# Opening of a fused attention and feed-forward kernel: queries begun on half of the contraction and half of the tokens, eight heads kept in float32 until their shift arrives

## The chip, the cores and the metric

One Trainium2 chip, one core. The metric is the device time of the whole kernel in microseconds (us). Runs of one kernel mostly agree within 0.2 us. A run also has a mean granted TensorE clock, where 1.000 means full clock throughout; it does not count the half-rate stretch at the very start.

PE is TensorE's matmul side and PEld its weight loads, DVE is VectorE, ACT is ScalarE, POOL is GpSimd, SP is the engine that issues the loads. "Head 4" means the fifth head; heads are counted from 0.

## The reference

Layer norm with a scale and a shift computed from a conditioning vector, attention of 32 query heads over the last 512 cached keys (4 key groups), a projection, a gated residual, then the same frame round a SwiGLU feed-forward. What matters here is the first line:

```python
mod = (silu(c) @ w_mod)            # six rows of 1024: sa (shift), ca (scale), ga, sb, cb, gb
h = layernorm(x) * (1 + ca) + sa
q = (h @ wq)                       # 2048 tokens, D = 1024, 32 heads of 128
p = softmax(q @ k.T * 128 ** -0.5) # 512 keys
x = x + ga * ((p @ v) @ wo)
# ... then h = layernorm(x) * (1 + cb) + sb, silu(h @ w_gate) * (h @ w_up) @ w_down, gated by gb
```

## The kernel before

The first 512 tokens can't be projected before the scale `ca` is there, and `ca` and `sa` must be computed from 2 MB of weights each. So the kernel transposes the normalised tokens, scales them, projects them without the shift, and adds `sa @ wq` (a "bias" per head) at the eviction. The kernel before does this for heads 0 to 3; the later heads read tokens that have had the shift added.

The contraction of 1024 runs in eight slices of 128 (`DT = 8`, `HK = 4`). `mm` is the only helper that issues matmuls, so nearly all matmuls have its line, L268, in every profile. `warm(n, b)` issues n dummy matmuls of 512 columns into bank b, which keep the TensorE clock up. The Trainium skill ("TensorE: Matmul & The Clock Gate", Part 1) says why one would: the array starts at half clock, goes to full after a busy window of some 3.4 us, and goes back after an idle one.

```python
            # ... x0..x3, all of the scale weights, wq group 0, shift weights, k0, wq group 1, ... are loaded in this order
            warm(7, WB)
            x_first(0)                         # transposes of 128 tokens, 8 slices
            warm(5, WB)
            x_first(1)
            for k in range(3):
                mod_ca(k)                      # 8 single-column matmuls: scale columns
                warm(1, WB)
            # ... x_first(2), x_first(3), mod_ca(3..7) with dummies between
            x_mod()                            # all 8 slices scaled, 512 tokens each, on DVE and ACT

            QB0 = [PVB, PVB + 1, SCB, QB]      # banks 5, 6, 0, 4
            for kc in range(DT):
                for h in range(LEAD + 1):      # heads 0 to 3
                    mm(bank(QB0[h]), wq_s[0][:, kc, h * P:(h + 1) * P], hT[0][:, kc, :], kc == 0, kc == DT - 1, ...)
                # ... shift columns mod_sa(0), mod_sa(1) after slices 3 and 6
            # ... mod_sa(2), dummies, mod_sa(3), key transposes of group 0, dummies
            for h in range(LEAD + 1):          # bias of heads 0 to 3, single columns
                for kc in range(DT):
                    mm(bank(SCB + 2, 1, 2 * h), wq_s[0][:, kc, h * P:(h + 1) * P], mod_bf[:, kc:kc + 1], ...)
            warm(5, SCB + 3)
            # ... shift added to the 8 slices; heads 0 to 3 evicted with their bias
```

The head loop, one turn per head. In these traces PE's matmuls come in the order of the program.

```python
            for i in range(1, NA + 2):
                # ... loads; key transposes of group i-1 in turns 2 to 4
                if i + LEAD < NA:
                    if i == 1:
                        scores(0)              # 4 matmuls into banks 0 to 3; ACT: 2 exponentials read them
                    qproj(i + LEAD, ...)       # 8 matmuls of 512 columns
                # ... in turns 7 to 14 one slice of another modulation column
                if 1 <= i - 1 < NA:
                    scores(i - 1)
                if 0 <= i - 2 < NA:
                    pv(i - 2)                  # 16 matmuls of 129 columns
```

Tracking: `T.op(engine, emit, reads, writes)` puts in a wait for the last write of each buffer it reads, whatever part of that buffer was written.

The softmax here doesn't subtract the row's maximum and nothing guards it: scores larger than these inputs give would overflow.

## Time and profile before

| | |
|---|---|
| Median of three runs | 1277.83 us (1277.81 to 1279.52) |
| Profiled run | 1279.7 us, span 1277.9 us, clock 1.000 |
| First query matmul, first scores, first exponential (profile) | 16.77, 29.24, 29.87 us |

Lines of the profile page of the kernel before: busy times of the engines with their share of the span, and the chain of work that ended last.

```profile
PE 1271.0 (99%) x7656; PEld 646.3 (51%) x7656; DVE 477.2 (37%) x883; ACT 340.3 (27%) x385; POOL 42.2 (3%) x102
...
PE 99%; DVE 0%; DMA 0%; ACT 0%; issue 0%; ACTq 0%
```

PE is the chain, so only PE time counts. A "busy" PE includes dummies and matmuls at half clock.

Lines of the timeline of the kernel before: start, duration, engine, line, operation, what it writes and reads, count, and in brackets how long the engine was idle before and what ended that.

```profile
8.77 0.15 PEld L268 LDWEIGHTS ps<-arena 128*128 128x128 bf16 x1 [0.28 <-issue]
...
9.20 0.15 PEld L268 LDWEIGHTS ps<-arena 128*128 128x128 bf16 x1 [0.28 <-issue]
...
16.77 3.89 PE L268 MATMUL ps<-arena 128*128 128x512 bf16 x16 [0.36 <-DVE arena L468]
...
29.24 1.02 PE L268 MATMUL ps<-arena 128*128 128x512 bf16 x4 [0.35 <-DVE arena L663]
...
29.87 1.02 ACT L690 ACTIVATE arena<-ps 128x1024 bf16<-128x1024 f32 x1 [0.26 <-PE ps L268]
```

At 9 us the dummies still start 0.43 us apart, which is half clock. Queries begin at 16.77 us and the first scores at 29.24 us.

### The profile page before, as it was taken

How to read it: one execution, taken by the hardware profiler on the slowest of the kernel's cores; microseconds unless marked ns; L12 is line 12 of the kernel's file. 1: busy time of each engine (PE TensorE's matmuls, PEld its weight loads, DVE VectorE, ACT ScalarE, POOL GpSimd, SP SyncE). 2: the span in 40 equal slices, each digit the busy share in tenths (PEclk: the TensorE clock that was granted, in tenths of full speed). 3: DMA queues.
4: the chain of work that ended last, by engine and by line, in shares of the span. 5: the costliest groups of instructions: out<-in, count | busy, mean ns of one | idle time of the engine just before them, and what ended most of it. 6: DMA issues, size and time to landing. Idle time of an engine off the chain costs nothing.

```text
span 1277.9 us, 17862 instructions
## 1 busy us (share of the span) xinstructions
PE 1271.0 (99%) x7656; PEld 646.3 (51%) x7656; DVE 477.2 (37%) x883; ACT 340.3 (27%) x385; POOL 42.2 (3%) x102
## 2 busy tenths in 40 slices
PE   8999999999999999999999999999999999999999
PEld 4565545555455564466544444444444444444444
DVE  3555324765247652265422322233222331222222
ACT  3555303555025550055510111011100111011100
POOL 1011000000000010000000000000000000000000
PEclk9999999999999999999999999999999999999999
DMA  9999403977018741065352964055421654035200
GB/s 319 234 239 235 104 1 72 200 139 165 3 22 186 153 104 42 2 131 112 71 149 81 291 221 132 23 145 162 134 72 45 197 146 132 17 114 166 67 9 25
DMA packets 234830, 155.31 MB, mean 122 GB/s; under 512 B 129024, under 2 KB 220032, under 8 KB 234752
## 3 DMA queue, kind: packets, MB, share of 16 engines
q1 hardware_dynamic: 176496, 95.45, 31.2%
q10 hardware_dynamic: 58256, 58.73, 14.6%
q8 instruction: 60, 0.98, 0.3%
q14 instruction: 18, 0.15, 0.1%
HBM read 119.54 MB, written 4.19 MB: 97 GB/s over the span
## 4 chain that ended last, share of the span: by engine, by line
PE 99%; DVE 0%; DMA 0%; ACT 0%; issue 0%; ACTq 0%
PE ps L268 99%; PE ps L272 0%; DMA x_res<-in_A_x_dram 0%; DVE st L396 0%; DVE arena L663 0%; ACT arena L471 0%; DVE arena L468 0%; DVE tmp L730 0%; DVE arena L732 0%; DVE nsc L407 0%; DVE mv L493 0%; DVE gain L448 0%; DVE mod_bf L462 0%; DVE bq L669 0%; ACTq L79 0%
## 5 line engine op out<-in xcount | busy, mean ns | idle before, releaser
L268 PE MATMUL ps<-arena 128*128 128x512 bf16 (+2 forms) x7383 | 1265.7, 334 | 3.0 <-POOL arena L389 2.2
L268 PEld LDWEIGHTS ps<-arena 128*128 128x128 bf16 x7383 | 636.1, 98 | 621.0 <-issue 3.5
L690 ACT ACTIVATE arena<-ps 128x1024 bf16<-128x1024 f32 x256 | 262.2, 1024 | 354.6 <-PE ps L268 343.0
L915 ACT ACTIVATE arena<-ps 128x512 bf16<-128x512 f32 x112 | 66.9, 597 | 506.4 <-PE ps L268 506.4
L916 DVE TENSOR_TENSOR arena<-ps,arena 128x512 bf16<-128x512 f32 x112 | 77.5, 692 | 276.2 <-PE ps L268 276.2
L730 DVE TENSOR_TENSOR tmp<-ps,rowb 128x512 f32<-128x512 f32 (+1 forms) x65 | 44.4, 683 | 319.1 <-PE ps L268 319.1
L609 DVE CAST arena<-ps 128x512 bf16<-128x512 f32 x124 | 85.8, 692 | 57.1 <-PE ps L268 57.1
L711 DVE TENSOR_TENSOR arena<-ps,rl 128x512 bf16<-128x512 f32 x128 | 88.5, 691 | 4.7 <-DVE rl L708 0.2
L708 DVE RECIPROCAL rl<-ps 128x4 f32<-128x4 f32 x128 | 23.3, 182 | 120.5 <-PE ps L268 120.5
L396 DVE BATCH_NORM_STATS2 st<-x_res 128x6 f32<-128x512 bf16 x62 | 42.3, 683 | 4.0 <-DMA x_res<-in_A_x_dram 3.8
L401 POOL TENSOR_SCALAR rstd<-mv 128x1 f32<-128x1 f32 x28 | 6.2, 222 | 895.6 <-DVE mv L400 895.6
L563 DVE SCALAR_TENSOR_TENSOR arena<-arena 128x1024 bf16<-128x1024 bf16 x24 | 29.1, 1215 | 0.0
L732 DVE TENSOR_TENSOR arena<-tmp,x_res 128x512 bf16<-128x512 f32 (+1 forms) x33 | 22.3, 676 | 1.1
L732 DVE TENSOR_TENSOR x_res<-tmp,x_res 128x512 bf16<-128x512 f32 x32 | 22.1, 692 | 1.1
L412 DVE TENSOR_SCALAR arena<-arena,gain,mod_bf 128x512 bf16<-128x512 bf16 x56 | 20.3, 405 | 0.0
L407 DVE TENSOR_SCALAR nsc<-x_res,mv,rstd 128x1024 bf16<-128x1024 bf16 x30 | 16.0, 534 | 0.0
L403 POOL TENSOR_TENSOR rstd<-rstd,mhalf 128x1 f32<-128x1 f32 x28 | 15.8, 565 | 2.3
L578 POOL TENSOR_SCALAR arena<-arena,c 128x128 bf16<-128x128 bf16 x24 | 14.4, 620 | 32.7 <-PE ps L268 32.4
L268 PEld LDWEIGHTS ps<-sc_bf,arena 128*128 128x128 bf16 x192 | 7.4, 97 | 3.4
L268 PE MATMUL ps<-sc_bf,arena 128*128 128x1 bf16 x192 | 7.5, 164 | 0.0
L400 DVE BATCH_NORM_AGGREGATE mv<-st 128x2 f32<-128x12 f32 x28 | 5.8, 208 | 1.0
L272 PE MATMUL ps<-arena,nsc 128*128 128x128 bf16 x16 | 2.1, 312 | 1.1 <-DVE nsc L407 1.1
(53 smaller groups left out, 42.7 us busy)
## 6 DMA issues: line engine op xcount, KB each, us to landing
arena<-in_A_wq_dram SPq DMA_DIRECT2D x31, 1024.0 KB, 5.7
arena<-in_B_w_gate_dram ACTq DMA_DIRECT2D x28, 1024.0 KB, 5.5
arena<-in_B_w_up_dram ACTq DMA_DIRECT2D x28, 1024.0 KB, 8.2
arena<-in_A_wo_dram SPq DMA_DIRECT2D x8, 1024.0 KB, 7.0
arena<-in_B_w_down_dram SPq DMA_DIRECT2D x7, 1024.0 KB, 8.1
out_dram<-arena SPq DMA_DIRECT2D x15, 256.0 KB, 2.0
x_res<-in_A_x_dram SPq DMA_DIRECT2D x3, 1024.0 KB, 7.9
arena<-in_w_mod_dram SPq DMA_DIRECT2D x8, 256.0 KB, 6.1
```

What stands on the lines that cost most here:

```text
L268: T.op(PE, lambda: TE.matmul(out_ap, lhsT, rhs, start=start, stop=stop, skip_group_check=skip), reads=reads, writes=[bank_buf])
L396: T.op(DVE, lambda: V.bn_stats(st_[sl][:, hf * 6:hf * 6 + 6], x_res[:, t, hf * 512:hf * 512 + 512]), reads=[B_x[t]], writes=[B_st[sl]])
L412: T.op(DVE, lambda: V.tensor_scalar(dst[:, dt, :], dst[:, dt, :], gain[gi][:, dt:dt + 1], mod_bf[:, ccol + dt:ccol + dt + 1], op0=ALU.mult ...
L563: T.op(DVE, lambda: V.scalar_tensor_tensor(mt[n % 2], mt[n % 2], 1.0, sc_row, op0=ALU.mult, op1=ALU.mult, accum_out=mcol[:, n:n + 1]), rea ...
L609: T.op(DVE, lambda: V.tensor_copy(qT_s[qs], bank(b)), writes=[PB[b], B_qT[qs]])
L690: T.op(ACT, lambda: A.activation(ex_s[es][:, 2 * kp:2 * kp + 2, :], banks2(SCB + 2 * kp), AF.Exp, scale=att_scale), writes=[PB[SCB + 2 * k ...
L708: T.op(DVE, lambda: V.reciprocal(rl[r][:, :].rearrange("p (a b) -> p a b", a=2), psap(PVB * 512 + P, [[512, 2], [130, 2]])), writes=both + ...
L711: T.op(DVE, lambda: V.tensor_tensor(o_s[os_].rearrange("p (a b) d -> p a b d", a=2), psap(PVB * 512, [[512, 2], [130, 2], [1, P]]), rlb, A ...
L730: T.op(DVE, lambda: V.tensor_tensor(tmp[s][:, 0:n], bank(b, n), rowb[ri][:, c0:c0 + n], ALU.mult), reads=[B_row[ri]], writes=[PB[b], B_tmp ...
L732: T.op(DVE, lambda: V.tensor_tensor(dst[:, c0:c0 + n], tmp[s][:, 0:n], x_res[:, t, c0:c0 + n], ALU.add), reads=[B_tmp[s], B_x[t]], writes= ...
L915: T.op(ACT, lambda: A.activation(sg_s[ss], bank(gb), AF.Silu), writes=[PB[gb], B_sg[ss]])
L916: T.op(DVE, lambda: V.tensor_tensor(guT[:, ft, :], bank(ub), sg_s[ss], ALU.mult), reads=[B_sg[ss]], writes=[PB[ub], B_gu[ft]])
```

## The change

Its intent is to begin real work earlier and to use the wait for the shift for projections, not for dummies.

- The scale weights come in two halves of the columns (1 MB each). The first half is enough for slices 0 to 3.
- Tokens 0 to 255 are scaled and projected (heads 0 to 2, slices 0 to 3) while tokens 256 to 511 are still being normalised.
- Heads 0 to 7 are projected without the shift. Each leaves PSUM as float32 (`q_raw`), and gets its bias in SBUF (`q_shifted`) when the shift column is there.
- Bias columns of heads 0 and 1 come before the first scores, those of heads 2 to 7 after them.
- In turns 2 to 8, heads 8 to 11 are projected in every second turn, as four projections are already done. Four slices of the next modulation column are moved into turn 7, which has no projection.
- Dummies fall from 35 to 19. A third query-weight slot takes group 2 early.

The diff, cut to its core:

```diff
-            for k in range(DT):
-                T.op(dq("q_wca%d" % k), lambda: SP.dma_start(wca[k], w_mod[k * P:(k + 1) * P, D:2 * D]), writes=[B_wca[k]])
+            def load_wca(hf):      # half of the columns, in four loads
...
-            warm(7, WB)
+            warm(12, WB)
             x_first(0)
-            warm(5, WB)
+            warm(3, WB)
+            for k in range(4):
+                mod_ca(0, k)
             x_first(1)
...
+            x_first(2, 0, HK)
+            x_gain(0)
+            x_mod(0, 0, 2 * P)
+            norm_last(0, 512)
+            norm(2, 2, 2, 512, 512)
...
+            BB = SCB + 3
+            QB0 = [QB, PVB, PVB + 1, SCB, SCB + 1, SCB + 2, QB, PVB]
+            def q_raw(h):          # float32 eviction to SBUF, DVE or ACT in turn
+            def q_bias_mm(h0, h1): # single columns into bank BB, then one copy to bq
+            def q_shifted(h):      # qT = qf + bq
...
+            for kc in range(HK):
+                for h in range(3):
+                    q_first(h, kc, 0, 2 * P)
+                if kc == 2:
+                    x_first(tl, 0, HK)
+                    x_mod(0, 2 * P, 2 * P)
+                    norm_last(512, 512)
+            for k in range(4):
+                mod_ca(1, k)
+            for kc in range(HK):
+                for h in range(3):
+                    q_first(h, kc, 2 * P, 2 * P)
+            x_first(2, HK, HK)
+            x_first(tl, HK, HK)
+            for k in range(4, DT):
+                mod_ca(1, k)
+            x_gain(1)
+            x_mod(1, 0, CH)
+            # ... head 3, slices 4 to 7 of heads 0 to 3, heads 4 to 7, with mod_sa and key transposes between
+            q_bias_mm(0, 2)
+            # ...
                     if i == 1:
                         scores(0)
-                    qproj(i + LEAD, PVB if i == 2 else QB)
+                        q_bias_mm(2, NQ0)
+                    if i > NQ0:
+                        qproj(i + LEAD)
+                    elif i % 2 == 0:
+                        qproj(NQ0 - 1 + i // 2)
```

## The prediction

> **What bounds the kernel.** The engine table gives PE 99% of a 1277.9 us span (DVE 37%, ACT 27%), and the chain that ended last is PE for 99%. So only PE time counts, and the change touches only the opening, before the ninth head. The timeline there: first transposes at 7.5 us, first query matmul at 16.77, first scores at 29.24. Query work in that stretch is 4 heads x 8 matmuls x 0.213 = 6.8 us. Much of the rest is dummies: 35 warming matmuls in the old prologue. From 29.24 on PE is gapless: heads take about 3.5 us each (3.7 to 3.9 with a key transpose or gate column), while ACT's two exponentials take 2.14.
>
> **What the change does.** It starts queries on half the contraction and half the tokens, so they need only half of the scale columns (1 MB loaded, not 2), and fills the wait for the shift column with heads 4 to 7 instead of dummies (19 left, not 35). It adds 8 float32 evictions (about 0.69 us each, split over DVE and ACT, off PE), 8 SBUF additions and 32 more single-column bias matmuls (16 of them take 0.40 us: 25 ns each, 0.8 us).
>
> **Estimated opening.** The DMA stretches hold 350 to 390 GB/s from 6 to 27 us; in the new order the first half of the scale should land near 10 us (the fourth of these loads now lands at about 10, the last near 12.7), the first query weights near 11.5, the shift columns by about 25. First query matmul: about 12 instead of 16.8, with gaps until about 16.5, as each half waits for DVE and ACT to scale it. Then 16 + 32 dense matmuls and the shift columns: first scores at about 29 to 30, as before, but with 8 heads projected. Worth 4 x 1.71 = 6.8 us.
>
> **Given back.** (1) Bias columns of heads 2 to 7: 48 x 25 ns = 1.2 us after the first scores. (2) They go to PSUM bank 3, which those scores have just filled: they wait until both exponentials (2 x 1.02 us) have read it, and PE has nothing else in order: about 1.7 us idle. (3) Heads 2 to 8 project only every second turn; a turn without it (1.75 us of scores and values) is shorter than 2.14 of ACT: some 0.5 us in all. (4) The keys of the second group come behind 1 MB more of weights, at about 32 us, when they are wanted: 0 to 1 us. About 6.8 - 3.4 - slips = 3 us left.
>
> **Prediction.** 1274.6 us; 8 in 10: 1271.5 to 1278.5. The rest (gate, up, down) doesn't change.
>
> **Clock.** In this trace matmuls of 512 columns start 0.43 us apart until about 11 us, 0.21 after. The Trainium skill ("TensorE: Matmul & The Clock Gate", Part 1) says the array starts at half rate and goes to full after a busy window of some 3.4 us; the trace agrees. Twelve dummies in a row without the present 1.1 us gap should bring full rate by 8 to 10 us. But the new stretch from 10 to 17 us is thin (short matmuls, waits, few dummies); should it fall back to half rate, the gain is gone.
>
> **What would show it.** Timeline: first query matmul near 12, first scores near 29 to 30; a PE gap of 1.5 to 2 us right after the first four score matmuls, released by the exponential; gaps of 0.2 to 0.5 us in odd turns until head 8; nothing different after, only shifted by 2 to 5 us. Wrong if: matmul spacing returns to 0.43 us; a wait on the key load of turn 2; the weights or shift columns landing after 27 us.
>
> Chances: faster by over 2% 0.01, within 2% 0.98, slower 0.01.

## The result

| | Before | After |
|---|---|---|
| Median, range, runs | 1277.85 us (1277.81 to 1279.52), 4 | 1280.16 us (1279.86 to 1281.05), 4 |
| Profiled run, its clock | 1279.7 us, 1.000 | 1281.05 us, 0.997 |
| First query matmul | 16.77 us | 11.31 us |
| First scores | 29.24 us | 30.83 us |

The ratio is 1.0016, with a 95% interval of 0.9999 to 1.0033. Ratios are the mean time of one kernel's fast runs over that of the other's fast runs of the same rounds, so they are not quite the ratio of the medians quoted. "Same" was forecast and came. But the size was not: a gain of 3.2 us was predicted, and the medians show a loss of 2.3 us, outside the stated range.

Lines of the profile page of the kernel after, as above:

```profile
PE 1262.2 (99%) x7542; PEld 646.7 (51%) x7684; DVE 479.9 (38%) x896; ACT 341.8 (27%) x390; POOL 42.0 (3%) x102
...
PE 98%; issue 1%; ACT 0%; DVE 0%; POOL 0%; POOLq 0%; ACTq 0%
```

PE is still the chain. The timeline of the kernel after, in the opening and the first turns:

```profile
11.05 0.98 ACT L492 ACTIVATE arena<-ps,gain_f 128x256 bf16<-128x256 bf16 x2
...
11.31 1.14 PE L268 MATMUL ps<-arena 128*128 128x256 bf16 x9 [0.57 <-DVE arena L489]
...
12.72 0.98 ACT L492 ACTIVATE arena<-ps,gain_f 128x256 bf16<-128x256 bf16 x2 [0.69 <-PE ps L272]
...
13.75 0.50 PE L268 MATMUL ps<-arena 128*128 128x256 bf16 x3 [1.07 <-ACT arena L492]
...
30.83 0.55 PEld L268 LDWEIGHTS ps<-arena 128*128 128x128 bf16 x4 [0.55 <-DVE arena L668]
...
31.47 2.14 ACT L755 ACTIVATE arena<-ps 128x1024 bf16<-128x1024 f32 x2
...
33.67 1.42 PE L268 MATMUL ps<-mod_bf,arena 128*128 128x1 bf16 x48 [1.80 <-ACT arena L755]
...
37.89 0.15 PEld L268 LDWEIGHTS ps<-arena 128*128 128x128 bf16 x1 [0.28 <-issue]
38.32 0.15 PEld L268 LDWEIGHTS ps<-arena 128*128 128x128 bf16 x1 [0.28 <-issue]
```

Three things are to be seen. After the first scores (30.83 us, here the load of their weights) PE waits 1.80 us for the exponential (L755), and then runs 48 single columns for 1.3 us, up to the next matmul at 34.95 us. At 38 us weight loads are again 0.43 us apart, which is half clock. And at 12.5 us three matmuls of the fourth slice wait 1.07 us for the *second* pair of ACT scalings (12.72 to 13.70), although the first pair, whose output they read, ended at 12.03.

The stretches of the kernel after say how long the clock was down. The column before the last two is the granted clock, mean of the stretch.

```profile
30.00:35.00 5.00, 3.14 (x57) 1.80 (x56) 3.14 (x11) 2.64 (x3) 0.00 (x0) 0.89 1.06 303
35.00:40.00 5.00, 4.78 (x18) 1.99 (x16) 1.68 (x4) 0.16 (x1) 0.00 (x0) 0.50 0.15 57
40.00:45.00 5.00, 4.95 (x51) 3.43 (x51) 2.80 (x8) 3.93 (x4) 0.00 (x0) 0.93 0.13 26
```

The clock lost is 5 us x (0.11 + 0.50 + 0.07) = 3.4 us, so it was at half for 6.8 us. That is two of the 3413 ns windows that the Trainium skill gives for this control ("TensorE: Matmul & The Clock Gate", Part 1).

### The profile page after: what moved, and what is told of

The parts are those of the page before. It is cut to its first block, busy times and chain, and to the rows that moved or that the text cites. A ratio compares the mean times of both kernels' runs of the same rounds, so it can differ in the third digit from the quotient of the medians.

```text
span 1279.3 us, 17804 instructions
## 1 busy us (share of the span) xinstructions
PE 1262.2 (99%) x7542; PEld 646.7 (51%) x7684; DVE 479.9 (38%) x896; ACT 341.8 (27%) x390; POOL 42.0 (3%) x102
## 4 chain that ended last, share of the span: by engine, by line
PE 98%; issue 1%; ACT 0%; DVE 0%; POOL 0%; POOLq 0%; ACTq 0%
PE ps L268 98%; ACT arena L755 0%; PE ps L272 0%; ACT arena L492 0%; DVE arena L489 0%; DVE rl L773 0%; DVE arena L668 0%; POOL arena L296 0%; DVE tmp L795 0%; DVE arena L797 0%; DVE gain L462 0%; DVE mod_bf L477 0%; DVE bq L663 0%; POOL arena L291 0%; POOL arena L290 0%
## 5 line engine op out<-in xcount | busy, mean ns | idle before, releaser
L755 ACT ACTIVATE arena<-ps 128x1024 bf16<-128x1024 f32 x256 | 261.8, 1023 | 354.5 <-PE ps L268 342.7
L642 DVE CAST arena<-ps 128x512 bf16<-128x512 f32 x120 | 83.0, 691 | 54.9 <-PE ps L268 54.9
L655 DVE COPY arena<-ps 128x512 f32<-128x512 f32 x4 | 2.7, 689 | 7.9 <-PE ps L268 7.9
```

Of the source, the lines that this page charges most:

```text
L642: T.op(DVE, lambda: V.tensor_copy(qT_s[qs], bank(b)), writes=[PB[b], B_qT[qs]])
L755: T.op(ACT, lambda: A.activation(ex_s[es][:, 2 * kp:2 * kp + 2, :], banks2(SCB + 2 * kp), AF.Exp, scale=att_scale), writes=[PB[SCB + 2 * k ...
```

## The experiments

Theory A: the hole after the first scores costs its own time and, in most runs, a fall of the clock. Rival B: the clock falls because of the thin stretch between 10 and 18 us, as the prediction feared, or the gain was never there. As the tests went on, two more suspects came up: the opening itself is late, and the profile that the prediction was read from was not typical.

Runs within one call share a chip and its runs of the kernel before: e1 to e4, then e0 and e5 to e7, then e8 to e11. All outputs were correct. A comparison of e5, e6 or e9 with e1, or of e10 with e7, goes from chip to chip, and the intervals of their ratios to before overlap; there the medians only suggest a size, and the traces have to bear it out.

| Run | What | Median us (range) | Clock of the runs | Ratio to before (95%) |
|---|---|---|---|---|
| e0_after | the change again | 1280.13 (1278.55 to 1280.93) | 1.000 x2, 0.999 x3 | 1.0009 (0.9997 to 1.0022) |
| e1_bank6 | bias into a free bank | 1277.03 (1276.54 to 1277.29) | 1.000 x5 | 0.9990 (0.9978 to 1.0003) |
| e2_fill | dummies in the hole | 1279.50 (1278.93 to 1279.93) | 1.000 x5 | 1.0009 (0.9997 to 1.0022) |
| e3_hole48 | before + the hole | 1282.74 (1282.55 to 1284.33) | 0.997 to 0.999 x4, 1.000 x1 | 1.0040 (1.0026 to 1.0053) |
| e4_hole1 | before + the wait alone | 1279.88 (1279.86 to 1283.24) | 1.000 x3, 0.999 x2 | 1.0023 (1.0010 to 1.0035) |
| e5_late | e1, no false wait | 1275.97 (1275.75 to 1276.56) | 1.000 x5 | 0.9981 (0.9969 to 0.9994) |
| e6_halves | e1, half a projection per turn | 1276.28 (1276.01 to 1278.84) | 1.000 x4, 0.997 x1 | 0.9986 (0.9974 to 0.9999) |
| e7_all | e5 + e6 + early second scale | 1274.46 (1274.17 to 1274.74) | 1.000 x5 | 0.9968 (0.9954 to 0.9981) |
| e8_before | before, another profile | 1279.16 (one run) | 1.000 | none |
| e9_tokens | e1, tokens not halved | 1276.30 (1276.10 to 1278.50) | 1.000 x4, 0.999 x1 | 0.9989 (0.9977 to 1.0002) |
| e10_all_tokens | e7, tokens not halved | 1274.72 (1274.63 to 1275.13) | 1.000 x5 | 0.9974 (0.9961 to 0.9988) |
| e11_warm10 | before, 10 first dummies | 1278.00 (1277.90 to 1278.27) | 1.000 x5 | 0.9999 (0.9987 to 1.0012) |

The kernel before had medians of 1277.92, 1278.24 and 1277.89 us, nine runs each.

### e1_bank6: the bias columns in a free bank

```diff
-            def q_bias_mm(h0, h1):
+            def q_bias_mm(h0, h1, BB=BB):
...
-                        q_bias_mm(2, NQ0)
+                        q_bias_mm(2, NQ0, PVB + 1)
```

> The changed kernel, with the bias columns of heads 2 to 7 put into PSUM bank 6, which is free, instead of bank 3, which the exponential still reads. Theory A (the hole after the first scores costs itself and a fall of the TensorE clock to half): the 1.8 us wait on the exponential is gone, the granted clock is 1.000 in every run, the time is 4 to 6 us below the changed kernel's 1280.2, so 1274 to 1276. Rival B (the clock fell because of the thin stretch from 10 to 18 us, or the gain was never there): clock still under 1.000, time 1278 or more.

Measured: 1277.03 us, clock 1.000 in all five runs, 3.1 us below the changed kernel. Lines of its timeline:

```profile
32.23 2.14 ACT L755 ACTIVATE arena<-ps 128x1024 bf16<-128x1024 f32 x2
32.46 1.34 PE L268 MATMUL ps<-mod_bf,arena 128*128 128x1 bf16 x48
33.67 0.38 PE L272 MATMUL ps<-arena 128*128 128x128 bf16 x4
34.10 3.10 PE L268 MATMUL ps<-arena 128*128 128x512 bf16 x21
```

The columns now run while the exponential does, with no wait before them. So the bank was what made PE wait at this place, and the change with this one word altered is 0.9 us better than before in the medians (an interval that just includes no difference). The mechanism of theory A holds; the size does not. I expected 4 to 6 us and got 3.1, and the kernel is still far from the 1273 us that the prediction's own sums give without the wait. Something else is missing. (A part is chance: the first query matmul of this profiled run came at 12.07 us, against 11.31 and 11.43 us in the two profiles of the changed kernel, and everything up to the first scores is later by that.)

### e2_fill: the wait kept, the array kept busy

```diff
                         scores(0)
+                        warm(8, PVB + 1)
                         q_bias_mm(2, NQ0)
```

> The changed kernel, with the wait left as it is but 8 dummy matmuls into the free bank 6 put between the first scores and the bias columns, so that PE is busy while it waits. Theory A: the clock stays at 1.000 and only the clock's share comes back, 1.7 us (one window of 3.4 us at half rate) to 3.4 us (two windows): 1276.8 to 1278.5. Rival B: as the changed kernel, 1280 with a clock of 0.997 to 0.999. Against the run before it tells apart the idle time (about 1.8 us) and the clock.

Measured: 1279.50 us; clock 1.000 in all five runs. The clock part of the expectation held, and the time missed: 0.7 us came back against the median of the changed kernel, not 1.7 or more. e0, the next run, explains it. There the changed kernel, unaltered, kept its clock in two of five runs and took 1278.55 and 1278.60 us. So the clock is worth 1.6 us, a little less than assumed, and e2 had a loss of its own of some 0.9 us against these two runs: in its profile the timeline is as e0's up to the end of the heads, and then one projection matmul waits for a transposing load.

The line of e2's timeline that shows it:

```profile
657.97 2.33 PE L268 MATMUL ps<-arena 128*128 128x512 bf16 x9 [0.68 <-DMA arena<-arena]
```

No other profile here has this wait at that place that I found; why e2 has it is open.

### e0_after: the changed kernel again

No edit.

> The changed kernel once more, on the same chip as the next three, for a comparison: 1279.8 to 1281.1, granted clock 0.997 to 0.999 in most runs.

Measured: 1278.60 and 1278.55 us with clock 1.000; 1280.13, 1280.20 and 1280.93 us with 0.999. Together with the first four runs: two of nine kept the clock, six ran at 0.999 (median 1280.17 us), and one at 0.997 (1281.05 us). The same program, then, pays 1.6 us when the clock is 0.999 in the mean and 2.5 us in the run whose profile shows it down for two windows; the six runs at 0.999 were not profiled. The profile of e0 is of a run that kept the clock, and is the cleanest picture of the waits:

```profile
31.59 2.14 ACT L755 ACTIVATE arena<-ps 128x1024 bf16<-128x1024 f32 x2
33.78 1.35 PE L268 MATMUL ps<-mod_bf,arena 128*128 128x1 bf16 x48 [1.80 <-ACT arena L755]
...
39.77 1.51 PE L268 MATMUL ps<-arena 128*128 128x512 bf16 x18 [0.24 <-ACT arena L755]
...
45.90 1.29 PE L268 MATMUL ps<-arena 128*128 128x512 bf16 x14 [0.46 <-ACT arena L755]
```

The 1.80 us wait is there, with no clock lost. The last two lines are turns 3 and 5, which have no projection: their scores wait for the exponential to leave the banks. (Start to start these two cost 0.40 and 0.62 us.)

### e3_hole48 and e4_hole1: the hole put into the kernel before

The same edit with N = 48 and N = 1, in the kernel before; the columns are not used.

```diff
                     if i == 1:
                         scores(0)
+                        for hh in range(N):
+                            mm(bank(SCB + 3, 1, 2 * hh), wq_s[1][:, hh % DT, 0:P], mod_bf[:, hh % DT:hh % DT + 1], ...)
                     qproj(i + LEAD, PVB if i == 2 else QB)
```

> The kernel before, with 48 single-column matmuls of no use written to bank 3 just after its first scores: the hole of the changed kernel without any other part of the change. Theory A: a wait of 1.8 to 2 us, 1.2 us of columns, and the clock falls to half for one or two windows of 3.4 us: 1277.8 plus 4.7 to 6.5, so 1282.5 to 1284.3, clock 0.997 to 0.999. Rival B: no fall of the clock, 1277.8 plus 3.1 = about 1281.

> The kernel before with a single such column after the first scores: the wait of 1.8 to 2 us alone, without the 1.2 us of single columns. If the wait alone makes the clock fall: 1277.8 plus 3.5 to 5.3, clock under 1.000. If wait and columns are needed together (a hole of some 3 us): clock 1.000 and 1277.8 plus 1.9 = about 1279.7. I expect the second.

Measured: e3 1282.74 us, 4.8 us over the kernel before, with the clock under 1.000 in four of five runs. e4 1279.88 us, 2.0 us over, in the three runs that kept the clock; the other two took 1282.85 and 1283.24 us at 0.999. The stretches of e3:

```profile
25.00:30.00 5.00, 2.98 (x41) 1.51 (x40) 3.18 (x10) 3.97 (x6) 0.00 (x0) 1.00 0.95 288
30.00:35.00 5.00, 4.46 (x60) 2.70 (x62) 0.15 (x1) 0.15 (x1) 0.00 (x0) 0.66 0.92 292
35.00:40.00 5.00, 4.99 (x39) 2.73 (x37) 2.77 (x6) 2.05 (x2) 0.00 (x0) 1.00 0.37 140
```

A granted clock of 0.66 over 5 us is 3.4 us at half. The opening of the kernel before, with its dense stretch full of dummies, loses its clock to the same hole. So the hole suffices (the fifth run of e3, 1282.74 us at a clock of 1.000, I can't explain), and Rival B is not needed for it. In the changed kernel too the hole is the main cause: of its nine runs seven lost clock, and of the fifteen of e1, e2 and e6, which have the same thin opening and no such hole, one did. In e4 two of five runs lost clock, none of the 27 runs of the kernel before: the wait alone seems to do it too, though these two runs were not profiled. I had expected that wait and columns were needed together, and that did not hold.

What decides whether a given run falls? The traces show a part of it. The clock's changes lie on a grid: between the first rise, the fall and the next rise there are 27.31 and 6.83 us in the changed kernel's profile and 23.89 and 3.41 us in e3, which is 8, 2, 7 and 1 times 3.41 us. So the grid can be laid back from the first rise. These are the steps of the grid around the hole: the one at whose end the clock fell in the changed kernel, the same in e3, then two each of e0 and e4, where it did not fall. The first number is the length, the second PE's busy time.

```profile
30.47:33.88 3.41, 1.55 (x14) 0.53 (x13) 2.80 (x10) 2.64 (x3) 0.00 (x0) 1.00 1.07 263
```

```profile
27.55:30.96 3.41, 1.52 (x31) 0.88 (x30) 1.14 (x3) 2.25 (x3) 0.00 (x0) 1.00 0.77 179
```

```profile
29.52:32.93 3.41, 2.41 (x25) 0.94 (x23) 2.69 (x10) 1.85 (x3) 0.00 (x0) 1.00 0.82 217
32.93:36.35 3.42, 2.51 (x57) 1.98 (x59) 1.16 (x5) 0.80 (x1) 0.00 (x0) 1.00 0.95 310
```

```profile
25.65:29.06 3.41, 2.29 (x18) 0.81 (x15) 2.48 (x7) 2.40 (x4) 0.00 (x0) 1.00 1.10 311
29.06:32.48 3.42, 2.23 (x15) 1.20 (x16) 0.28 (x1) 1.02 (x1) 0.00 (x0) 1.00 0.98 310
```

Where the hole lay within one step, PE was busy for 45% of it and the clock fell; where the edge of a step cut the hole in two, both steps were busy for 65 to 73%, and it did not. The thinnest step of the opening, 59% busy in e1 and 62% in the changed kernel, brought no fall either. Where the grid lies differs from run to run. This is read from four traces and is no measured threshold, but it is a plain reason why one program falls in some runs and not in others.

One more thing was in these two traces. Before the hole they run the instructions of the kernel before, but faster than its profile shows. Lines of e4's timeline:

```profile
27.34 1.02 PE L268 MATMUL ps<-arena 128*128 128x512 bf16 x4 [0.35 <-DVE arena L663]
27.96 2.14 ACT L690 ACTIVATE arena<-ps 128x1024 bf16<-128x1024 f32 x2 [0.26 <-PE ps L268]
30.25 0.16 PE L268 MATMUL ps<-mod_bf,arena 128*128 128x1 bf16 x1 [1.89 <-ACT arena L690]
```

First scores are at 27.34 us, not at 29.24. The kernel before was 1.9 us faster in its opening than the profile that the prediction was read from.

### e8_before and e11_warm10: why the first profile was late

e8 is the kernel before without any edit. e11 is this:

```diff
-            warm(7, WB)
+            warm(10, WB)
```

> The kernel before, unchanged, for another profile of it. Its profile came from a run of 1279.7 us, while two runs in three take 1277.9. Expected in a run of 1277.9: full clock by 5 to 8 us, first exponential at 28.0 us and not 29.87. In a run of 1279.3: as in the first profile.

> The kernel before with 10 dummies in place of 7 in its first row, so that the 1.1 us PE gap at 6.4 to 7.5 us closes. If the late full clock (11.5 us in the profile of before, 5 to 7 us in the two traces of before with a hole) makes its slow runs of 1279.3 (about one in three): all five runs at 1277.7 to 1278.2. If the slow runs have another cause: one or two of five at 1279 or more.

Measured: e8 1279.16 us, again a slow one; first exponential at 29.33 us. e11 1277.90 to 1278.27 us in all five runs, first exponential at 28.05 us. Stretches of the first profile of before, of e8, of e4 and of e11, in that order; the count in brackets after the first number is of matmuls:

```profile
5.00:10.00 5.00, 3.90 (x16) 1.67 (x15) 4.27 (x10) 2.74 (x5) 2.70 (x7) 1.00 1.00 356
```

```profile
5.00:10.00 5.00, 4.24 (x17) 1.82 (x16) 4.05 (x10) 3.08 (x5) 2.96 (x8) 1.00 0.98 346
```

```profile
5.00:10.00 5.00, 3.54 (x39) 1.89 (x38) 4.05 (x10) 3.03 (x5) 3.04 (x8) 1.00 1.01 345
```

```profile
5.00:10.00 5.00, 4.75 (x39) 2.36 (x37) 4.05 (x10) 2.88 (x5) 3.04 (x8) 1.00 1.00 348
```

Between 5 and 10 us the two slow runs get through 16 and 17 matmuls, the two fast ones through 39. The clock column says 1.00 in all four, because the trace has no clock event before the first rise; the rate must be read from the matmuls. By the trace's own events (the packed trace of a run has them) full clock came at 11.5 us (first exponential 29.87), at 10.7 (29.33), at 7.1 in e3 (28.02), at 6.8 in e11 (28.05) and at 5.2 in e4 (27.96). The three early rises go with first exponentials within 0.1 us of each other, the two late ones with exponentials 1.3 to 1.9 us later.

The gap that seven dummies leave before the first transposes (1.1 us in the first profile) fits as the cause: in the two slow traces the step of the grid that holds it was busy for 68 and 78%, and the rise came only at the end of the next step, which was busy throughout. With ten dummies, no run of five was slow. But of the 27 runs of before only 7 were at 1279.0 or more, so five fast runs in a row would come by luck about once in five. That e11 cures it is not shown. What is shown is that the profile of before was a slow run.

### e5_late: the false wait of the fourth slice

In the changed kernel the transposes and the scaling of tokens 256 to 511 are written down ahead of the fourth slice's matmuls. The buffer of a slice is one buffer for both halves of the tokens, so these matmuls wait for the later scaling. e5 has bank 6, and this:

```diff
-                if kc == 2:
+                if kc == HK - 1:
                     x_first(tl, 0, HK)
                     x_mod(0, 2 * P, 2 * P)
```

> The changed kernel with the bias columns in bank 6, and the transposes and the scaling of the second half of the tokens put after the fourth slice of the contraction, not before it. In the changed kernel that slice's first-half matmuls wait at 12.5 to 13.75 us for the scaling of the second half, which they don't need: the program counts both halves of a slice as one buffer. If that wait delays the opening: the 1.24 us gap goes, first scores 1.0 to 1.3 us earlier, time 1.0 to 1.3 us below the run with bank 6 alone (1277.0), so about 1275.7 to 1276.1. If the opening is held up elsewhere (loads, the scaling itself): no change, 1277.0.

Measured: 1275.97 us, 1.06 us below the median of e1. The timeline of e5:

```profile
11.70 1.47 PE L268 MATMUL ps<-arena 128*128 128x256 bf16 x12 [0.57 <-DVE arena L489]
13.01 0.39 PE L272 MATMUL ps<-arena 128*128 128x128 bf16 x4
...
31.02 1.34 PE L268 MATMUL ps<-mod_bf,arena 128*128 128x1 bf16 x48
32.90 0.40 PE L272 MATMUL ps<-arena 128*128 128x128 bf16 x4 [0.54 <-DMA arena<-in_A_k_cache_dram]
```

All twelve matmuls of the first half run in one go and the wait is gone. From the first query matmul to the first exponential it takes 19.1 us here (11.70 to 30.78), and 20.2 us in the changed kernel (11.31 to 31.47), in e0 and in e1: so the false wait is worth 1.1 us of opening, whatever the medians add. A part is handed back at once: turn 2 now comes before the keys of the second group have landed, and PE waits 0.54 us for them. This is the load that the prediction worried about; in the changed kernel as made, it is hidden because PE is late.

### e6_halves: half a projection in each turn

With bank 6:

```diff
-                    elif i % 2 == 0:
-                        qproj(NQ0 - 1 + i // 2)
+                    elif i % 2 == 1 and i < NQ0:
+                        qproj_mm(NQ0 + i // 2, QB, 0, HK)
+                    elif i % 2 == 0:
+                        hq = NQ0 - 1 + i // 2
+                        qproj_mm(hq, QB, HK, DT)
+                        # ... eviction to qT as in qproj
```

> The changed kernel with the bias columns in bank 6, and the projections of heads 8 to 11 cut into two halves of four matmuls, one half in each turn, in place of a whole one in every second turn. If the turns without a projection starve for the exponential (waits of 0.40 and 0.63 us in the trace at turns 3 and 5): these waits go, 0.8 to 1.1 us below 1277.0, so 1275.9 to 1276.2. If they are made good later anyway: 1277.0.

Measured: median 1276.28 us, 0.75 us below the median of e1, a little short of the expectation. PE's waits on the exponential in the first turns are gone from its timeline. One of its five runs took 1278.84 us at a clock of 0.997, without the hole. That run was not profiled; where its clock fell is open. The thin opening, which is still there, remains a suspect: in the trace that was kept, PE is busy for only 49% of the 3.41 us from 10.90 to 14.31 us, close to the 45% at which the clock fell elsewhere, though no step of that run's grid lay just so.

### e9_tokens and e10_all_tokens: the halving of the tokens undone

e9 starts from e1, e10 from e7. Both scale all 512 tokens of the first four slices at once and use 512-column matmuls (e10 also leaves the fourth slice until after the second scaling); in e9:

```diff
-            x_first(2, 0, HK)
+            norm_last(0, 512)
+            x_first(2, 0, HK)
+            x_first(tl, 0, HK)
             x_gain(0)
-            x_mod(0, 0, 2 * P)
-            norm_last(0, 512)
+            x_mod(0, 0, CH)
...
-                    q_first(h, kc, 0, 2 * P)
-                # ... (the block at kc == 2, and the second loop over the other 256 tokens)
+                    q_first(h, kc, 0, CH)
```

> The changed kernel with the bias columns in bank 6, and the halving of the tokens undone: one scaling of all 512 tokens for the first half of the contraction, 512-column matmuls after it. If halving the tokens pays as the change means it to: slower than the run with bank 6 alone (1277.0), 1277.5 or more. If its false wait (1.24 us) and its extra instructions cost more than the earlier start gains: 0.5 to 1.5 us faster, 1275.5 to 1276.5. I expect the second.

> The best kernel so far (bank 6, no false wait, halves of projections, early second scale) with the halving of the tokens undone. There the false wait is gone, so this tells what the halving by itself is worth: 1274.5 to 1275.2 if the 0.3 to 0.6 us earlier start is worth anything, 1274.2 to 1274.5 if the second loads (first query weights at 11.1, second at 15.6 us) set the pace anyway.

Measured: e9 1276.30 us, 0.7 us below the median of e1, while the ratios to before, 0.9989 and 0.9990, are the same. The trace speaks for the medians: the first exponential comes at 30.94 us in e9, at 31.47 and 31.59 us in the changed kernel and e0. So in the change as made, halving the tokens seems to cost more than it gains; that is the false wait, for in e5, halved but without it, the exponential comes at 30.78 us. e10 1274.72 us against e7's 1274.46; the intervals of their ratios to before overlap, and the first exponentials come at 30.41 and 30.32 us. With the false wait gone, the halving is worth at most some tenths of a microsecond, and these runs don't settle whether it is worth anything.

### e7_all: the three repairs together, and the second scale earlier

e1, e5 and e6, and the second half of the scale columns moved between slices 1 and 2 of the second half of the tokens, so that their scaling runs under matmuls:

```diff
-            for kc in range(HK):
+            for kc in range(2):
                 for h in range(3):
                     q_first(h, kc, 2 * P, 2 * P)
             x_first(2, HK, HK)
             # ... mod_ca(1, 4..7), x_gain(1), x_mod(1, 0, CH)
+            for kc in range(2, HK):
+                for h in range(3):
+                    q_first(h, kc, 2 * P, 2 * P)
```

> Bank 6, the fourth slice before the second half of the tokens, halves of projections, and also the second half of the scale columns computed before the last two slices of the second half of the tokens, so that the scaling runs under matmuls (the 0.5 us gap at 17.5 us). If the three losses add up: about 1.7 us of opening and 1.0 us of turns below 1277.0: 1274.0 to 1274.7, clock 1.000. If they hide one another: 1275.5 or more.

Measured: 1274.46 us, clock 1.000 in all five runs, ratio 0.9968 (0.9954 to 0.9981). It beats both kernels: by 3.8 us the kernel before, and by 5.7 us the changed kernel. The repairs add up, as far as the medians can say. The early second scale was not run alone; the trace gives it 0.5 us, for from the first query matmul (11.75 us) to the first exponential it now takes 18.6 us, against e5's 19.1. From its timeline:

```profile
13.77 0.89 PE L268 MATMUL ps<-arena 128*128 128x256 bf16 x6
...
15.35 2.97 PE L268 MATMUL ps<-arena 128*128 128x256 bf16 x15
...
30.32 2.14 ACT L758 ACTIVATE arena<-ps 128x1024 bf16<-128x1024 f32 x2
30.55 1.34 PE L268 MATMUL ps<-mod_bf,arena 128*128 128x1 bf16 x48
31.97 0.81 PE L268 MATMUL ps<-arena 128*128 128x512 bf16 x3
```

There is no wait in these lines.

## Why the prediction was wrong

Two steps failed: the opening was not "as before" but 3.6 us longer, and the wait on bank 3 was not idle time only: seven of nine runs lost clock, and with the wait gone or filled (e1, e2) none of ten did. The rest is of tenths of a microsecond.

What held:

- PE bounds the kernel, and nothing after the first turns changed. In the profiles the distance to the kernel before is 1.31 us at head 16 and still 1.31 us in the feed-forward.
- The first query matmul came at 11.31 us ("about 12"). Eight heads are projected at the first scores.
- Given-back (2), the wait on bank 3, was foreseen at about 1.7 us, and is 1.80 us in the trace.
- Given-back (1), 48 columns at 25 ns, took 1.2 us (e0).
- Full clock by 8 to 10 us: it came at 5.6 and 6.6 us in the two profiles of the changed kernel.

What failed, in the prediction's own words:

- **"first scores at about 29 to 30, as before".** Both halves of this were off. "As before" was 29.24 us, read from a profile of a 1279.7 us run, whereas the base of the sum was the median, 1277.83 us. A run at the usual level has its first scores at 27.34 us (e4). That is 1.9 us of the predicted gain that the kernel before already had. The changed kernel was late as well: 30.83 us in its profile, 30.95 by the same reckoning in e0. The false wait (1.07 us idle, 1.1 us of opening by e5) was in the diff, and I read the order of the calls without asking which buffer they mark as written.
- **"about 1.7 us idle", counted as idle time only.** The fall of the clock was foreseen, but for "the new stretch from 10 to 17 us", where the profiles show full clock. In the one profile of the changed kernel that shows a fall, it came in the hole that the prediction had itself found. It costs 1.6 us in most runs (e0), without the hole it is gone (e1, e2), and the hole alone, in another kernel, brings it about (e3).
- **"some 0.5 us in all"** for the turns without a projection: the two waits cost 0.40 and 0.62 us, about 1.0 us, and halving the projections got 0.75 us back (e6).
- **"0 to 1 us"** for the late keys: nothing in the changed kernel, 0.54 us in e5, once PE was earlier.

The sum, for runs that keep the clock. The opening is 30.95 - 27.34 = 3.6 us longer, the four projections already done are worth 6.8 us, the bias columns cost 1.2, the wait 2.0 (start to start), the starved turns 1.0. That makes 3.6 - 6.8 + 1.2 + 2.0 + 1.0 = 1.0 us slower. Measured: 1278.55 against 1277.9, or 0.65 us. So the terms are good to some 0.4 us. With the clock's 1.6 us the sum is 2.6, and the medians show 2.3. The prediction had about 0 for the 3.6, nothing for the 1.6 and half of the 1.0: 3.6 + 1.6 + 0.5 = 5.7 us, against the 5.6 us between 1274.6 and 1280.16; that this fits to 0.1 us is luck.

So where the gain went: half of the 6.8 us was spent in a longer opening, and the rest turned into one new wait, a fall of the clock that this wait sets off, and two starved turns. Most of this does not lie in the idea. With the bank, the order and the projections put right (e7) the same idea is worth 3.8 us. But e7's first exponential, at 30.32 us, is still 2.3 us later than the 28.0 us of the kernel before at its usual level: eight heads don't fit into the opening for the price of four, even then.

What stays open: how thin a step of the grid has to be for the clock to fall (45% busy did it, 59% did not); why single runs of e6 and e9 fell without the hole, and why one of e3 was slow at full clock; e2's wait at 658 us; and whether halving the tokens is worth anything.

## What to carry to other kernels

Before a profile's times are set against a median, look whether the profiled run was at the median; here 1.9 us of a 3.2 us forecast was that difference. When PE is the bound and work is moved to a new place in its order, list for each moved matmul which bank it writes, who reads that bank last, and which *buffer*, not which bytes, its wait is bound to. A PE hole of 2 us, with or without matmuls of one column after it, may cost more than 2 us: where it lay within one 3.41 us step of the clock's grid, the clock was at half for 3.4 or 6.8 us after it.

## What the Trainium skill lacked or had wrong

- "TensorE: Matmul & The Clock Gate", Part 1 and the table of "Why this matters for your kernels", gives idle gaps over about 3 us as what sends the clock back. Here a 1.8 us wait followed by 48 single columns went with a fall in seven of nine runs (the changed kernel), a 1.9 us wait with them in four of five (e3), and a 1.9 us wait between dense stretches in two of five (e4, not profiled). The window needn't be idle: the two whose end brought the fall were busy for 45%. The page's window length agrees with the lost clock: 3.4 us at half in e3, 6.8 us in the changed kernel's profile.
- The same section gives about 4 us of sustained activity to the first rise, within 0.5 us from run to run, warns that the count of cold matmuls varies, and says that the ramp is under 1% of a kernel and not to be fitted. In one and the same opening, whose first matmul is at 2.2 us and in which PE then waits once before its transposes (1.1 us in the first profile), full clock came at 5.2, 7.1, 10.7 and 11.5 us, and the late ones cost 1.3 to 1.9 us. This is small as a share (0.1%), but as large as many changes to a tuned kernel.
- No page that I read says that a granted clock of 1.00 in the first microseconds of a trace does not mean full clock: it stood at 1.00 where matmuls started 0.43 us apart.
